# Loads of 64-bit weights by GpSimd's queue, a third merged attention block, and the last 512 tokens in two runs

## The chip, the cores and the metric

One core of a Trainium2 chip runs the whole program in one launch. The metric is the time of one execution on the device in microseconds, as the median of several runs. The engines are TensorE (PE, matmuls; its weight loads are PEld), VectorE (DVE), ScalarE (ACT), GpSimd (POOL) and SyncE (SP, which here only issues transfers).

## The reference, cut to what matters

```python
# r, k, v, w: (2, 8, 768, 48); u: (8, 48); all float32
for t in range(768):                                   # per batch and head
    y[t]  = r[t] @ (state + outer(u * k[t], v[t]))
    state = w[t][:, None] * state + outer(k[t], v[t])
x = y as (1536 tokens, 384)
h = x @ w_in                  # 384 -> 2048; w_in, w_out are float64
x = (h * sigmoid(h)) @ w_out  # 2048 -> 384
P = exp(logits - max), logits = x @ w_gate             # 8 experts
8 times: P /= P.sum(1); P /= P.sum(0); P *= 1536 / 8
out = sum over e of P[:, e] * (relu(x @ w1[e]) @ w2[e])  # 384 -> 1024 -> 384
```

## The kernel before, in words

**Attention** goes in 24 units: 6 blocks of 256 tokens (three for each batch entry) times 4 pairs of heads; unit i is block i // 4, pair i % 4. A unit has four parts: `attn_a` (decay products by scans on VectorE), `attn_b` (scores on TensorE, masked on VectorE), `attn_c` (states) and `attn_d` (outputs y on TensorE, copied by ScalarE at line 338 and sent by DMA to the block's x1). Units below NS = 8, the first two blocks, take a merged form: one scan (line 296) over a unit's four chunk states, whose multipliers, the decay operands `tot`, ScalarE writes at line 291; all else on VectorE and ScalarE. Units 8 and up take a plain form: four chained steps (line 313), two products (line 316), more and smaller instructions on VectorE, and two products on GpSimd (lines 194, 204).

**First dense layer.** 2048 hidden columns are 16 f-tiles. The first 512 tokens are steps 0 to 15, tokens 512 to 1023 two runs of 256 (steps 16 to 31 and 32 to 47), the last 512 tokens steps 48 to 63. Step s runs `m_l1` (9 matmuls and silu; line 476 forms the remainder of g on VectorE) and `m_l2` of step s - 2 (9 matmuls). Every float32 operand is split into a rounded part and a remainder, so each product takes three matmuls.

**Weights.** w_in and w_out are float64 and come as pairs of 32-bit words, in 32 pieces of 384 columns. SP issues each into one of four raw buffers. `narrow` makes float32 of it by three integer operations on VectorE (lines 127, 129, 130); ScalarE rounds (line 104) and VectorE, or GpSimd for pieces 8 to 31, subtracts (line 106). A gate (line 82) is a one-element copy on ScalarE into a raw buffer out of a unit's x tile, so that the transfer behind it waits for parts b of units 4, 5 and 6. Expert weights (64 pieces of 768 columns, float32) use the same buffers.

**Order.** The program is written in the order of `run`: units 0 to 7 first, then the steps, with pieces split by `wcurve` and attention parts by `curve`. x1 of blocks 2, 3, and 4 and 5 together is split at steps 16, 32 and 48. Each engine's order comes from a scheduler in the compiler that goes by this order where it can. Each engine then works in order. In the expert phase (192 steps of 21 matmuls) `w_range` reads w and the double weights again to test their range, one part a step.

Of the kernel before, what the change touches and what calls it, by code (L numbers as in the profile page):

```python
# [5 lines left out]
F32 = mybir.dt.float32  # L6
F32R = mybir.dt.float32r
# [19 lines left out]
LN = 64 + D  # L27
NS = 2 * NP
C_MASK = 0
# [25 lines left out]
class Pipeline:  # L55
# [4 lines left out]
    def setup_weights(self):  # L60
        self.pieces = []
        win, wout, w1, w2 = (self.ins[n] for n in ("moe_w_in", "moe_w_out", "moe2_w1", "moe2_w2"))
        for f in range(16):
            for kind, src in (("a", win), ("b", wout)):
                self.pieces.append((kind, f // 8, f % 8, src[:, f * HP:(f + 1) * HP].bitcast(I32)))
        for e in range(E):
            for j in range(4):
                for kind, src in (("a", w1), ("b", w2)):
                    self.pieces.append((kind, 2 + e, 2 * j, src[e][:, j * PIECE:(j + 1) * PIECE]))
        self.n_dma = self.n_split = 0  # L70
        self.raw, self.wt, self.gates = {}, {}, {}

    def dma_pieces(self, n):
        nc = self.nc
        n = min(n, len(self.pieces))
        while self.n_dma < n:
            i = self.n_dma
            src = self.pieces[i][3]
            t = self.raw_p.tile([128, PIECE], F32, tag="raw", name="raw")
            gate = self.gates.get(i)  # L80
            if gate is not None:
                nc.scalar.copy(t[0:1, 0:1], gate)
            nc.sync.dma_start(out=t.bitcast(I32) if i < N64 else t, in_=src)
            self.raw[i] = t
            self.n_dma += 1

    def split_pieces(self, n):
        nc = self.nc
        n = min(n, len(self.pieces))
        while self.n_split < n:  # L90
            i = self.n_split
            self.dma_pieces(i + 1)
            kind, u, f, _ = self.pieces[i]
            raw = self.raw.pop(i)
            if i >= N64 or f % 2 == 0:
                pool = self.wa_p if kind == "a" else self.wb_p
                self.wt[kind, u, f // 2] = (pool.tile([128, PIECE], F32R, tag="hi", name="whi"),
                                            pool.tile([128, PIECE], F32R, tag="lo", name="wlo"))
            hi, lo = self.wt[kind, u, f // 2]
            if i < N64:  # L100
                o = (f % 2) * HP
                hi, lo = hi[:, o:o + HP], lo[:, o:o + HP]
                raw = self.narrow(i, raw)
            nc.scalar.copy(hi, raw)  # L104
            eng = nc.vector if i < N64 and not K['wl_pool'][0] <= i < K['wl_pool'][1] else nc.gpsimd
            eng.tensor_sub(lo, raw, hi.bitcast(F32))  # L106
            self.n_split += 1
            self.dma_pieces(self.n_split + 3)

    def narrow(self, i, raw):  # L110
# [60 lines left out]
    def attn_a(self, i):  # L171
# [7 lines left out]
        d1 = self.d1[i % 2]  # L179
        if i == 2:  # L180
            zek = self.aux[0:LN, 0:2 * WPAD + BLK]
            zf, ef = (zek[:, o:o + WPAD].rearrange("p (c t) -> p c t", c=4) for o in (0, WPAD))
            kz = zek[:, 2 * WPAD:].rearrange("p (c t) -> p c t", c=4)
        else:
            zf = self.sc_p.tile([LN, 4, CH + 2], F32, tag="zf", name="zf")
            ef = self.sc_p.tile([LN, 4, CH + 2], F32, tag="ef", name="ef")
            kz = self.sc_p.tile([LN, 4, CH], F32, tag="kz", name="kz")
        zff = zf.rearrange("p c t -> p (c t)")
# [31 lines left out]
    def attn_b(self, i):  # L220
        nc = self.nc
        if i < NS:
            self.warm(K['wm'])
# [49 lines left out]
    def attn_c(self, i):  # L273
        nc = self.nc
        blk, p = divmod(i, NP)
        b, q = divmod(blk, BPS)
        if i < NS:
            self.warm(K['wm'])
# [4 lines left out]
        if i < NS:  # L283

            uv = self.attn_bank("u", i)[0:LN, 0:6 * D].rearrange("p (e c) -> p e c", c=6)
            for c in range(4):
                for lo in (0, 64):
                    nc.tensor.matmul(uv[lo:lo + D, :, c + 1], lhsT=kt[lo:lo + 64, c, :], rhs=lv[lo:lo + 64, 1, c, :],
                                     start=True, stop=True)
            tot = self.tot[i % 2]  # L290
            nc.scalar.copy(tot[:, :, 0:4], st["zf"][:, :, 1].rearrange("p (o c) -> p o c", o=1).to_broadcast([LN, D, 4]))
            if q == 0:
                nc.vector.memset(uv[:, :, 0], 0.0)
            else:
# [24 lines left out]
    def attn_d(self, i):  # L319
# [21 lines left out]
        for s in range(2):  # L341
            for off, n, c, pp in dense_runs(2 * p + s):
                (nc.scalar if i < NS else nc.sync).dma_start(out=self.x1[blk][pp:pp + n, c, :], in_=ys[64 * s + off:64 * s + off + n, :])
        if p > 0 and blk < 2:
# [20 lines left out]
    def attn_x(self, i):  # L365
        return self.x[i % 4 if i < NS else i % 2]

    def attn_bank(self, kind, i):
        if i < NS and i % 2:
            return self.banks[{"m": 0, "u": 3, "y": 4}[kind]]  # L370
# [17 lines left out]
    def attn_tiles(self):  # L388
        self.d1 = [self.ac_p.tile([LN, 4, CH + 2], F32, name=f"d1{j}") for j in range(2)]
        self.x = [self.ac_p.tile([128, 2, 4, CH], F32, name=f"x{j}") for j in range(2)]  # L390
        xx = self.x2_p.tile([128, 2, 2, 4, CH], F32, name="xx", tag="x2_1")
# [3 lines left out]
        o = 2 * WPAD + BLK  # L395
        self.tot = [self.aux[0:LN, o + j * 6 * D:o + (j + 1) * 6 * D].rearrange("p (e c) -> p e c", c=6) for j in range(2)]
        self.oneb = self.ac_p.tile([128, 128], F32R, name="oneb")
# [199 lines left out]
    def w_range(self):  # L597
        nc = self.nc
        sm = self.sm_p
        n = NT * DM // (128 * PIECE)  # L600
        mm = sm.tile([128, 2, n], F32, name="wmm")
        for i in range(n):
            t = self.raw_p.tile([128, PIECE], F32, tag="raw", name="wt")
            nc.sync.dma_start(out=t, in_=self.ins["w"][:, i * PIECE:(i + 1) * PIECE])
            yield
# [11 lines left out]
        for i in range(N64):  # L617
            t = self.raw_p.tile([128, PIECE], F32, tag="raw", name="wh64")
            nc.sync.dma_start(out=t.bitcast(I32), in_=self.pieces[i][3])
# [19 lines left out]
    def run(self):  # L639
        tc, nc = self.tc, self.nc  # L640
        with ExitStack() as ctx:
# [16 lines left out]
            self.wb_p = pool("wb", 8)  # L658
            self.raw_p = pool("raw", 4)
            self.x2_p = pool("x2", 1)  # L660
# [37 lines left out]
            ticks.sort(key=lambda t: (t[2] >= NS, t[0], -t[2]))  # L698
            pos = [0]

            def attn_to(n):
                while not gen and pos[0] < len(ticks) and (ticks[pos[0]][2] < NS or ticks[pos[0]][0] < n):
                    _, fn, i = ticks[pos[0]]
# [24 lines left out]
            x1_at = {6: 2, 12: 3, 28: 4, 38: 5}  # L728
            split_at = {16: (2,), 32: (3,), 48: (4, 5)}

# [7 lines left out]
            for i in range(len(steps) + 2):  # L738
                if i < len(steps):
                    s = steps[i]  # L740
                    if s[0] == "m":
# [9 lines left out]
                        attn_to(at(curve, i + 1))  # L751
                        if tb == 2:
                            if f == 0:
# [13 lines left out]
                if i >= 2:  # L767
                    s = steps[i - 2]
                    if s[0] == "m":
                        _, tb, o, n, f = s  # L770
                        self.m_l2(tb, o, n, f)
                        if f == 15 and tb == 2:
                            self.logits(2)
# [86 lines left out]
```

## Time and profile before

| | us |
|---|---|
| median of 3 runs (1153.33 to 1156.07) | 1155.81 |
| the profiled execution | 1154.07 |
| its span, first to last instruction | 1152.3 |
| TensorE busy | 1115.0 |
| VectorE, ScalarE, GpSimd busy | 494.7, 319.5, 185.4 |
| first matmul of step 16, of step 32, of the expert phase | 161.3, 208.3, 332.7 |

A row of the order of time has the start and the duration in us, the engine and line, the operation, the tiles (out<-in, buffer numbers left out) and shapes; in brackets the idle time of the engine ahead of it and what ended it. Matmuls are pipelined, so that their durations overlap and only the distance of their starts tells their price. A clock of 1.00 is 2.4 GHz, 0.50 is 1.2 GHz.

### The profile page before, as it was taken

How to read it: one execution, taken by the hardware profiler on the slowest of the kernel's cores; microseconds unless marked ns; L12 is line 12 of the kernel's file. 1: busy time of each engine (PE TensorE's matmuls, PEld its weight loads, DVE VectorE, ACT ScalarE, POOL GpSimd, SP SyncE). 2: the span in 40 equal slices, each digit the busy share in tenths (PEclk: the TensorE clock that was granted, in tenths of full speed). 3: DMA queues.
4: the chain of work that ended last, by engine and by line, in shares of the span. 5: the costliest groups of instructions: out<-in, count | busy, mean ns of one | idle time of the engine just before them, and what ended most of it. 6: DMA issues, size and time to landing. Idle time of an engine off the chain costs nothing.

```text
span 1152.3 us, 16926 instructions
## 1 busy us (share of the span) xinstructions
PE 1115.0 (97%) x6928; PEld 989.9 (86%) x6928; DVE 494.7 (43%) x985; ACT 319.5 (28%) x613; POOL 185.4 (16%) x137
## 2 busy tenths in 40 slices
PE   7778999998999999999999999999999999999997
PEld 7656789996888999999999999899999999899996
DVE  7699967894233321222224522432442253222221
ACT  3243334444541243113112311311331241111110
POOL 0136511211440031004003100400310040000000
PEclk8659999999999999999999999999999999999999
DMA  5565512211230021003103400510340050000000
GB/s 139 163 194 155 154 44 72 74 43 49 83 84 13 1 56 54 1 15 83 42 1 101 133 1 17 150 53 1 94 126 1 23 159 26 1 1 1 28 28 30
DMA packets 32087, 71.81 MB, mean 62 GB/s; under 512 B 4752, under 2 KB 11904, under 8 KB 32000
## 3 DMA queue, kind: packets, MB, share of 16 engines
q1 hardware_dynamic: 30912, 69.86, 21.4%
q8 instruction: 56, 0.92, 0.3%
q10 hardware_dynamic: 1088, 0.79, 0.2%
q14 instruction: 31, 0.25, 0.1%
HBM read 65.91 MB, written 2.36 MB: 59 GB/s over the span
## 4 chain that ended last, share of the span: by engine, by line
PE 76%; ACT 0%; DVE 0%; issue 0%; DVEq 0%
PE bank L579 12%; PE bank L581 12%; PE bank L563 12%; PE bank L564 12%; PE bank L580 12%; PE bank L562 11%; PE bank L487 1%; PE bank L468 1%; PE bank L489 1%; PE bank L488 1%; PE bank L469 1%; PE bank L470 1%; ACT x2h L522 0%; DVE acc L592 0%; PE bank L507 0%; PE bank L549 0%
## 5 line engine op out<-in xcount | busy, mean ns | idle before, releaser
L568 DVE SCALAR_TENSOR_TENSOR hl<-bank,hh 128x512 fp32r<-128x512 f32 x192 | 132.2, 689 | 413.4 <-ACT hh L567 413.3
L579 PE MATMUL bank<-whi,hh 128*128 128x384 f32 x768 | 258.8, 337 | 0.0
L580 PE MATMUL bank<-wlo,hh 128*128 128x384 f32 x768 | 258.4, 336 | 0.0
L581 PE MATMUL bank<-whi,hl 128*128 128x384 f32 x768 | 257.6, 337 | 0.0
L567 ACT ACTIVATE hh<-bank 128x512 fp32r<-128x512 f32 x192 | 114.4, 596 | 483.1 <-PE bank L564 476.3
L564 PE MATMUL bank<-x2h,wlo 128*128 128x512 f32 x576 | 228.0, 396 | 0.0
L563 PE MATMUL bank<-x2l,whi 128*128 128x512 f32 x576 | 227.4, 395 | 0.0
L562 PE MATMUL bank<-x2h,whi 128*128 128x512 f32 x576 | 224.3, 389 | 0.0
L106 POOL TENSOR_TENSOR wlo<-raw,whi 128x768 fp32r<-128x768 f32 x64 | 119.4, 1870 | 579.3 <-ACT whi L104 551.2
L579 PEld LDWEIGHTS bank<-whi,hh 128*128 128x128 f32 x768 | 144.3, 188 | 9.2 <-issue 0.6
L580 PEld LDWEIGHTS bank<-wlo,hh 128*128 128x128 f32 x768 | 144.2, 188 | 8.0
L581 PEld LDWEIGHTS bank<-whi,hl 128*128 128x128 f32 x768 | 144.1, 188 | 1.4
L564 PEld LDWEIGHTS bank<-x2h,wlo 128*128 128x128 f32 x576 | 108.0, 188 | 22.4
L563 PEld LDWEIGHTS bank<-x2l,whi 128*128 128x128 f32 x576 | 108.0, 188 | 17.4
L562 PEld LDWEIGHTS bank<-x2h,whi 128*128 128x128 f32 x576 | 108.2, 188 | 17.0
L104 ACT CAST whi<-raw 128x768 fp32r<-128x768 f32 x64 | 53.6, 837 | 90.7 <-PE bank L563 54.1
L468 PE MATMUL bank<-x1h,whi 128*128 128x512 f32 (+1 forms) x192 | 68.1, 359 | 7.3 <-ACT x1h L357 7.3
L592 DVE SCALAR_TENSOR_TENSOR acc<-bank,P,acc 128x384 f32<-128x384 f32 x84 | 47.8, 610 | 58.0 <-PE bank L581 58.0
L469 PE MATMUL bank<-x1l,whi 128*128 128x512 f32 (+1 forms) x192 | 67.9, 353 | 0.3 <-DVE x1l L358 0.3
L488 PE MATMUL bank<-gl,whi 128*128 128x512 f32 (+1 forms) x192 | 66.4, 346 | 1.4 <-DVE gl L476 1.4
L470 PE MATMUL bank<-x1h,wlo 128*128 128x512 f32 (+1 forms) x192 | 67.4, 351 | 0.0
L476 DVE TENSOR_TENSOR gl<-g,gh 128x512 fp32r<-128x512 f32 (+1 forms) x64 | 44.2, 693 | 53.4 <-ACT gh L475 37.6
(163 smaller groups left out, 1176.5 us busy)
## 6 DMA issues: line engine op xcount, KB each, us to landing
raw<-in_moe_w_dram SPq DMA_DIRECT2D x64, 384.0 KB, 3.2
at<-in_att_dram SPq DMA_DIRECT2D x16, 484.0 KB, 3.6
raw<-in_moe_w_in_dram SPq DMA_DIRECT2D x16, 384.0 KB, 3.4
raw<-in_moe_w_out_dram SPq DMA_DIRECT2D x16, 384.0 KB, 3.4
wh<-in_moe_w_in_dram SPq DMA_DIRECT2D x16, 384.0 KB, 3.2
wh<-in_moe_w_out_dram SPq DMA_DIRECT2D x16, 384.0 KB, 3.2
at<-in_att_dram SPq DMA_DIRECT2D x7, 339.5 KB, 3.7
wt<-in_w_dram SPq DMA_DIRECT2D x6, 384.0 KB, 3.2
```

Of the source, the lines that this page charges most:

```text
L106: eng.tensor_sub(lo, raw, hi.bitcast(F32))
L468: nc.tensor.matmul(ps, lhsT=wh, rhs=xh[:, d, :], start=(d == 0), stop=False)
L469: nc.tensor.matmul(ps, lhsT=wh, rhs=xl[:, d, :], start=False, stop=False)
L470: nc.tensor.matmul(ps, lhsT=wl, rhs=xh[:, d, :], start=False, stop=(d == 2))
L562: nc.tensor.matmul(ps, lhsT=wh, rhs=xh[:, d, :], start=(d == 0), stop=False)
L563: nc.tensor.matmul(ps, lhsT=wh, rhs=xl[:, d, :], start=False, stop=False)
L564: nc.tensor.matmul(ps, lhsT=wl, rhs=xh[:, d, :], start=False, stop=(d == 2))
L567: nc.scalar.activation(hh, ps, ACTF.Relu)
L568: nc.vector.scalar_tensor_tensor(hl, ps, 0.0, hh.bitcast(F32), op0=ALU.max, op1=ALU.subtract)
L579: nc.tensor.matmul(ps, lhsT=hh[:, sl], rhs=wh, start=st, stop=False)
L580: nc.tensor.matmul(ps, lhsT=hh[:, sl], rhs=wl, start=False, stop=False)
L581: nc.tensor.matmul(ps, lhsT=hl[:, sl], rhs=wh, start=False, stop=sp)
```

## The change

The double weights come in 16 pieces of 768 columns. GpSimd issues their loads and makes the gate copies, now behind parts b of units 3 and 5. They have three raw buffers: two of the pool and one that takes the place of the decay operands (tag x2_0); expert weights share the pool's two in pairs. All 16 remainders are formed on VectorE. The third block (units 8 to 11) takes the merged form; the first two blocks have four decay operands instead of two, the third block one of its own. The last 512 tokens are two runs of 256, with x1 of blocks 4 and 5 split at steps 48 and 64, and attention spread accordingly. The range test reads in pieces of 1536 columns and starts one expert later.

```diff
-NS = 2 * NP
+N4 = 2 * NP
+NS = 3 * NP
-N64 = 32
-HP = PIECE // 2
+N64 = 16
-K = {'tk': (4, 0, 2, 4, 6), 'wr': (3, 0), 'wl_pool': (8, 32), 'wm': 1, 'gate': (4, 5, 6)}
+K = {'tk': (4, 0, 2, 4, 6), 'wr': (4, 0), 'wm': 1, 'gate': (3, 5)}
...
-            t = self.raw_p.tile([128, PIECE], F32, tag="raw", name="raw")
-            gate = self.gates.get(i)
-            if gate is not None:
-                nc.scalar.copy(t[0:1, 0:1], gate)
-            nc.sync.dma_start(out=t.bitcast(I32) if i < N64 else t, in_=src)
+            if i < N64:
+                if i % 3 < 2:
+                    t = self.raw_p.tile([128, 2, PIECE], F32, tag="raw", name="raw")
+                else:
+                    if i == 2:
+                        self.raw64 = self.x2_p.tile([128, 2, PIECE], F32, tag="x2_0", name="raw")
+                    t = self.raw64
+                gate = self.gates.get(i)
+                if gate is not None:
+                    nc.gpsimd.tensor_copy(t[0:1, 0, 0:1], gate)
+                nc.gpsimd.dma_start(out=t.rearrange("p s n -> p (s n)").bitcast(I32), in_=src)
+            else:
+                if i % 2 == 0:
+                    self.raw2 = self.raw_p.tile([128, 2, PIECE], F32, tag="raw", name="raw")
+                t = self.raw2[:, i % 2]
+                nc.sync.dma_start(out=t, in_=src)
...
-            eng = nc.vector if i < N64 and not K['wl_pool'][0] <= i < K['wl_pool'][1] else nc.gpsimd
-            eng.tensor_sub(lo, raw, hi.bitcast(F32))
+            (nc.vector if i < N64 else nc.gpsimd).tensor_sub(lo, raw, hi.bitcast(F32))
             self.n_split += 1
-            self.dma_pieces(self.n_split + 3)
+            self.dma_pieces(self.n_split + 2)
...
-            tot = self.tot[i % 2]
+            tot = self.tot[i % 4 if i < N4 else 4]
...
-        self.tot = [self.aux[0:LN, o + j * 6 * D:o + (j + 1) * 6 * D].rearrange("p (e c) -> p e c", c=6) for j in range(2)]
+        self.tot = [self.aux[0:LN, j * 6 * D:(j + 1) * 6 * D].rearrange("p (e c) -> p e c", c=6) for j in range(4)] + [late]
...
-        n = NT * DM // (128 * PIECE)
+        n = NT * DM // (128 * 2 * PIECE)
...
-            for tb, o, n in ((0, 0, 512), (1, 0, 256), (1, 256, 256), (2, 0, 512)):
+            for tb, o, n in ((0, 0, 512), (1, 0, 256), (1, 256, 256), (2, 0, 256), (2, 256, 256)):
...
-            curve = [(0, 32), (15, 51), (31, 67), (46, 104), (NM, 104)]
-            wcurve = [(0, 6), (13, 32), (NM, 32)]
-            split_at = {16: (2,), 32: (3,), 48: (4, 5)}
+            curve = [(0, 32), (15, 51), (31, 67), (47, 83), (63, 104), (NM, 104)]
+            wcurve = [(0, 4), (13, 16), (NM, 16)]
+            split_at = {16: (2,), 32: (3,), 48: (4,), 64: (5,)}
```

Elsewhere tests of `i < NS` that choose banks, x tiles, warm-up matmuls, the queue of x1's stores and the order of parts become `i < N4`.

## Rows read from the trace of the kernel before

**Rows 1.** Windows by stage: length, busy (count) by engine, PEclk, DMA share, GB/s.
```profile
34.00:80.00 46.00, 32.44 (x374) 25.34 (x371) 38.12 (x87) 15.23 (x43) 10.31 (x13) 0.59 0.64 193
80.00:161.00 81.00, 74.72 (x432) 57.40 (x430) 70.19 (x137) 32.49 (x65) 37.74 (x29) 0.92 0.44 129
161.00:208.00 47.00, 47.00 (x503) 43.60 (x503) 35.44 (x85) 19.36 (x52) 7.48 (x8) 1.00 0.21 61
208.00:260.00 52.00, 52.00 (x656) 48.51 (x655) 47.26 (x127) 21.86 (x62) 9.32 (x12) 1.00 0.21 61
260.00:277.00 17.00, 13.29 (x99) 9.15 (x98) 8.84 (x19) 7.54 (x16) 1.84 (x1) 0.90 0.05 13
344.00:1148.00 804.00, 800.44 (x4046) 724.61 (x4038) 249.79 (x445) 178.48 (x296) 88.97 (x49) 1.00 0.16 44
```
**Rows 2.** VectorE in order of time: start, duration, line, tiles, idle time before.
```profile
23.32 0.76 DVE L296 TENSOR_TENSOR_SCAN ss<-bank,aux 112x288 f32<-112x288 f32 x1
...
27.78 0.76 DVE L296 TENSOR_TENSOR_SCAN ss<-bank,aux 112x288 f32<-112x288 f32 x1
...
35.68 0.36 DVE L127 TENSOR_SCALAR cv<-raw 128x384 int32<-128x384 int32 x1 [3.25 <-DMA raw<-in_moe_w_in_dram]
...
45.09 0.36 DVE L127 TENSOR_SCALAR cv<-raw 128x384 int32<-128x384 int32 x1 [3.50 <-DMA raw<-in_moe_w_out_dram]
...
46.03 0.75 DVE L296 TENSOR_TENSOR_SCAN ss<-bank,aux 112x288 f32<-112x288 f32 x1
...
66.65 0.75 DVE L296 TENSOR_TENSOR_SCAN ss<-bank,aux 112x288 f32<-112x288 f32 x1
...
77.97 1.23 DVE L358 TENSOR_TENSOR x1l<-x,x1h 128x256 fp32r<-128x256 f32 x1
```
**Rows 3.** ScalarE in order of time, unit 4's end and unit 5's gate.
```profile
41.32 0.19 ACT L82 COPY raw<-x 1x1 f32<-1x1 f32 x1 [2.03 <-DVE x L264]
41.41 0.36 ACT L338 COPY ys<-bank 112x256 f32<-112x256 f32 x1
```
**Rows 4.** VectorE's groups from 0 to 260 us: count, busy us, mean ns, idle.
```profile
L130 DVE SCALAR_TENSOR_TENSOR cv<-raw,cv 128x384 int32<-128x384 int32 x32 | 20.7, 651 | 0.1
...
L129 DVE SCALAR_TENSOR_TENSOR cv<-raw,cv 128x384 int32<-128x384 int32 x32 | 18.9, 598 | 0.3
...
L127 DVE TENSOR_SCALAR cv<-raw 128x384 int32<-128x384 int32 x32 | 14.1, 446 | 10.8 <-DMA raw<-in_moe_w_in_dram 4.7 <-DMA raw<-in_moe_w_out_dram 3.5 <-POOL wlo L106 2.6
...
L476 DVE TENSOR_TENSOR gl<-g,gh 128x256 fp32r<-128x256 f32 x31 | 13.3, 429 | 5.4 <-ACT gh L475 5.3
...
L106 DVE TENSOR_TENSOR wlo<-cv,whi 128x384 fp32r<-128x384 f32 x8 | 4.3, 542 | 0.0
```
**Rows 5.** Single lines: count, shortest/median/longest ns, first and last start.
```profile
L127 DVE TENSOR_SCALAR cv<-raw x32: 323/348/1175, 35.7 to 127.5; 128x384 int32<-128x384 int32 x32
...
L130 DVE SCALAR_TENSOR_TENSOR cv<-raw,cv x32: 532/545/1381, 37.3 to 132.4; 128x384 int32<-128x384 int32 x32
...
L106 POOL TENSOR_TENSOR wlo<-raw,whi x64: 1835/1846/2271, 274.9 to 949.6; 128x768 fp32r<-128x768 f32 x64
L106 POOL TENSOR_TENSOR wlo<-cv,whi x24: 997/1120/6118, 69.0 to 135.7; 128x384 fp32r<-128x384 f32 x24
```
**Rows 6.** TensorE in order of time: steps 14, 16 and 21.
```profile
150.71 0.39 PE L468 MATMUL bank<-x1h,whi 128*128 128x512 f32 x1
...
152.53 0.39 PE L470 MATMUL bank<-x1h,wlo 128*128 128x512 f32 x1
...
161.30 0.39 PE L468 MATMUL bank<-x1h,whi 128*128 128x256 f32 x1
...
188.19 0.28 PE L468 MATMUL bank<-x1h,whi 128*128 128x256 f32 x1
...
189.15 0.28 PE L470 MATMUL bank<-x1h,wlo 128*128 128x256 f32 x1
```
**Rows 7.** DMA issues: count, KB each, median us to landing.
```profile
raw<-in_moe_w_in_dram SPq DMA_DIRECT2D x16, 384.0 KB, 3.4
```

More of the change, by code (lines that the diff above doesn't have):

```diff
@@ L62, in setup_weights @@
         win, wout, w1, w2 = (self.ins[n] for n in ("moe_w_in", "moe_w_out", "moe2_w1", "moe2_w2"))
-        for f in range(16):
+        for g in range(8):
             for kind, src in (("a", win), ("b", wout)):
-                self.pieces.append((kind, f // 8, f % 8, src[:, f * HP:(f + 1) * HP].bitcast(I32)))
+                self.pieces.append((kind, g // 4, 2 * (g % 4), src[:, g * PIECE:(g + 1) * PIECE].bitcast(I32)))
         for e in range(E):
@@ L179, in attn_a @@
         d1 = self.d1[i % 2]
[L180 to L187, printed above, removed]
+        zf = self.sc_p.tile([LN, 4, CH + 2], F32, tag="zf", name="zf")
+        ef = self.sc_p.tile([LN, 4, CH + 2], F32, tag="ef", name="ef")
+        kz = self.sc_p.tile([LN, 4, CH], F32, tag="kz", name="kz")
         zff = zf.rearrange("p c t -> p (c t)")
@@ L221, in attn_b @@
         nc = self.nc
-        if i < NS:
+        if i < N4:
             self.warm(K['wm'])
@@ L342, in attn_d @@
             for off, n, c, pp in dense_runs(2 * p + s):
-                (nc.scalar if i < NS else nc.sync).dma_start(out=self.x1[blk][pp:pp + n, c, :], in_=ys[64 * s + off:64 * s + off + n, :])
+                (nc.scalar if i < N4 else nc.sync).dma_start(out=self.x1[blk][pp:pp + n, c, :], in_=ys[64 * s + off:64 * s + off + n, :])
         if p > 0 and blk < 2:
@@ L365, in attn_x @@
     def attn_x(self, i):
-        return self.x[i % 4 if i < NS else i % 2]
+        return self.x[i % 4 if i < N4 else i % 2]
     def attn_bank(self, kind, i):
-        if i < NS and i % 2:
+        if i < N4 and i % 2:
             return self.banks[{"m": 0, "u": 3, "y": 4}[kind]]
@@ L390, in attn_tiles @@
         self.x = [self.ac_p.tile([128, 2, 4, CH], F32, name=f"x{j}") for j in range(2)]
-        xx = self.x2_p.tile([128, 2, 2, 4, CH], F32, name="xx", tag="x2_1")
+        xx = self.x2_p.tile([128, 3 * 512], F32, name="xx", tag="x2_1")
+        late = xx[0:LN, 1024:1024 + 6 * D].rearrange("p (e c) -> p e c", c=6)
+        xx = xx[:, 0:1024].rearrange("p (j s c t) -> p j s c t", j=2, s=2, c=4)
         self.x += [xx[:, 0], xx[:, 1]]
@@ L599, in w_range @@
         sm = self.sm_p
-        n = NT * DM // (128 * PIECE)
+        n = NT * DM // (128 * 2 * PIECE)
         mm = sm.tile([128, 2, n], F32, name="wmm")
         for i in range(n):
-            t = self.raw_p.tile([128, PIECE], F32, tag="raw", name="wt")
-            nc.sync.dma_start(out=t, in_=self.ins["w"][:, i * PIECE:(i + 1) * PIECE])
+            t = self.raw_p.tile([128, 2 * PIECE], F32, tag="raw", name="wt")
+            nc.sync.dma_start(out=t, in_=self.ins["w"][:, i * 2 * PIECE:(i + 1) * 2 * PIECE])
             yield
@@ L617, in w_range @@
         for i in range(N64):
-            t = self.raw_p.tile([128, PIECE], F32, tag="raw", name="wh64")
+            t = self.raw_p.tile([128, 2 * PIECE], F32, tag="raw", name="wh64")
             nc.sync.dma_start(out=t.bitcast(I32), in_=self.pieces[i][3])
@@ L658, in run @@
             self.wb_p = pool("wb", 8)
-            self.raw_p = pool("raw", 4)
+            self.raw_p = pool("raw", 2)
             self.x2_p = pool("x2", 1)
@@ L697, in run @@
                     ticks.append((K["tk"][0] * i + o, fn, i))
-            ticks.sort(key=lambda t: (t[2] >= NS, t[0], -t[2]))
+            ticks.sort(key=lambda t: (t[2] >= N4, t[0], -t[2]))
             pos = [0]
             def attn_to(n):
-                while not gen and pos[0] < len(ticks) and (ticks[pos[0]][2] < NS or ticks[pos[0]][0] < n):
+                while not gen and pos[0] < len(ticks) and (ticks[pos[0]][2] < N4 or ticks[pos[0]][0] < n):
                     _, fn, i = ticks[pos[0]]
@@ L751, in run @@
                         attn_to(at(curve, i + 1))
-                        if tb == 2:
+                        if tb == 2 and o == 256:
                             if f == 0:
@@ L771, in run @@
                         self.m_l2(tb, o, n, f)
-                        if f == 15 and tb == 2:
+                        if f == 15 and tb == 2 and o == 256:
                             self.logits(2)
```

23 lines of the change are left out of this document (9 added, 14 removed).

## The prediction

> **What bounds the kernel now.** I read the page first, then the busy times by stage, then the order of work on single engines where a stage loses time. By stage [rows 1]: from 344 to 1148 us TensorE is busy 800.4 of 804 us at the full clock. That is the expert phase, and of it the change touches only the loads of raw weights and the range test, both off TensorE. I leave it as it is. All that can move lies ahead of 344 us. From 161 to 260 us TensorE is busy without a break; from 260 to 277 it is idle for 3.7 us and its granted clock is 0.90. From 34 to 80 us it is busy 32.4 of 46 us at a clock of 0.59 (a mixture of 1.2 and 2.4 GHz), and from 80 to 161 us VectorE is busy 70.2 of 81. So the front is held by a chain through VectorE, the middle by TensorE, and one seam (260 to 277) by a wait.
>
> The front's chain is seen in VectorE's order of work [rows 2]. Each merged attention unit ends its state in one scan of line 296. Units 2 and 3 finish 4.46 us apart (23.32, 27.78). Then unit 5 comes only at 46.03 and unit 7 at 66.65: four gaps of 9.72 on average. The cause stands between them: VectorE, which works in order, sits 3.25 and 3.50 us before line 127, waiting for a piece of double weights that has not landed. ScalarE adds to it [rows 3]: its gate copy of line 82 waits 2.03 us for VectorE's select of the next unit, and the copy of y (line 338) that ends the unit before stands behind it. Only after unit 7 can the first 512 tokens be complete: its x1 remainder ends at 77.97 + 1.23 = 79.2 us, 12.55 us after the scan began. From there to the start of step 16 (161.3, [rows 6]) are 82 us for the first 512 tokens.
>
> **The sum is made** against the profiled execution: 1154.07 us, a span of 1152.3 and 1.8 around it. The median of the three runs is 1.7 us more, which I add at the end. A measurement of this kernel tells from no change about 0.3%, 3.5 us.
>
> **Part 1: gates and loads by GpSimd, the third buffer, four decay operands (first two blocks).** The gate copies leave ScalarE. Of sixteen pieces only two can be on their way before unit 7's scan: the third buffer is the memory of the four decay operands (tag x2_0) and comes free with that scan, and on GpSimd's queue piece 3 stands behind piece 2. So VectorE can be held at most twice in units 4 to 7. If nothing held it, unit 7's scan would begin at 27.78 + 4 x 4.46 = 45.6 us. If the conversion of both pieces falls inside the chain, it costs two times 3.25 us (next part): 52.1. If VectorE also waits 3.4 us for each of the two landings, as it did [rows 2]: 58.9. I take 52, because attention stands first in program order but pieces fill gaps, and no gate holds ScalarE any more. The gain is 66.65 - 52 = 14.6 us, with bounds 7.7 and 21. The four decay operands end a wait of ScalarE that only mattered between units; I count it as nothing, since VectorE is the slower there. Loads on SP (attention inputs, x1 stores) no longer queue behind waits for raw buffers; nothing in the rows shows that they were late, so nothing.
>
> **Part 2: wider pieces, remainder on VectorE.** Per half piece VectorE now does 0.35 (line 127), 0.54 and 0.54 us undisturbed [rows 5] but 0.45, 0.60 and 0.65 on average [rows 4], since GpSimd's subtractions (24 of them, 1.12 us each at the median, [rows 5]) run beside it and single instructions stretch to 1.38 us. All narrowing and 8 subtractions: 14.1 + 18.9 + 20.7 + 4.3 = 58.0 us. For 768 columns: a subtraction takes 0.43 us for 256 columns and 0.54 for 384 [rows 4], so some 0.9 us for 768; lines 129 and 130 have 384's time in common with it, so 0.9 each; line 127 between 0.35 and 0.70, I take 0.55. A piece is 0.55 + 3 x 0.9 = 3.25 us, sixteen are 52.0: 6 less than now, though all subtractions move to VectorE. The upper bound is two halves each, 2 x (0.35 + 3 x 0.54) = 3.9 us, 63 in all, 5 more than now. GpSimd's 24 subtractions vanish, and with them the stretching of other instructions.
>
> **Part 3: third block merged.** A plain unit costs VectorE at most 5.4 us: (47.26 - 16 x 0.43 for g's remainders - 6 x 0.43 for x1's) / 7 units from 208 to 260 us [rows 1, 4]. A merged one is at most 4.46 [rows 2], its share of x1's remainder with it, so some 4.1. Four units save 5 us. TensorE pays: a plain unit is (52.0 - 16 x 2.16) / 8 = 2.2 us; a merged one issues 48 matmuls by the code where a plain one issues 28, so between 2.2 and 2.2 x 48 / 28 = 3.8; I take 3.2, 4 us more in all.
>
> **Parts 1 to 3 together, the first 512 tokens.** They are complete at 52 + 12.6 = 64.6 us (now 79.2). From there TensorE needs 16 x 4.1 (18 matmuls 0.2275 us apart, [rows 6]) + 4 x 3.2 = 78 us. VectorE needs 13 pieces (three are done by then), 42 us, 16 remainders of g at 0.65 (worked out as above for 512 columns), 10, four merged units, 16, and 3 us of the next: 72. TensorE's floor is now 65.6 + 8.8 = 74, of which the measured 82 is 8 more. After: 78 plus 2, since VectorE no longer lags as much; 80, with bounds 78 and 88 (the same 8 and the upper price of Part 2). That is 2 us less (bounds -4 and +6). The transfers are covered: a half piece lands 3.4 us after issue [rows 7], 193 GB/s went through at a busy share of 0.64 [rows 1], and three buffers turn around in 15 us at 5 us a piece. If the cover is gone, see the slower rival.
>
> **Part 4: last 512 tokens as two runs, attention spread to step 63.** A 256-column step costs 18 x 0.12 = 2.16 us, a 512-column one 4.1 [rows 6]: two for one cost 0.24 more, sixteen times 3.84 us. The wait at step 48 goes: 3.7 us idle, and (1 - 0.90) x 17 = 1.7 us of clock, 5.4 together. Attention of the last two blocks only moves, its TensorE time is the same. What is late next are the seams: unit 19's last part is issued in step 46 for a need in step 48, unit 23's in step 58 for step 64. Net -1 us; bounds -1.6 (all of it) and +7 (a wait of 3 us at both seams on top of 3.84). The expert weights are now split in 16 steps of 2.16 us; GpSimd's 8 subtractions of 1.85 us [rows 5] fit in 35 us. Expert phase with two raw buffers of pairs, and half as many range-test loads: nothing, covered by TensorE; VectorE is busy 250 of 804 us there.
>
> **Sum.** 1154.07 - 14.6 - 2 - 1 = 1136.5, plus 1.7: 1138 us. Its own range, half of the parts' bounds added up (-3.2 - 1 - 0.3 and +3.5 + 4 + 4): 1133 to 1150.
>
> **The rivals.**
> A, landings still hold VectorE, and longer. Place: lines 127 of pieces 0 and 1, ahead of scans 4 to 7. For it: twice the bytes per piece, on a queue that this trace has no transfer of. Against it: two holds instead of three or more, and ScalarE free. Scan at 59 instead of 52, so 1138 + 7 = 1145 us.
> On this hold the Trainium skill, "SBUF — State Buffer", section "SBUF: two separate sides", speaks against the change: a transfer issued from GpSimd has its descriptors written by that engine, and VectorE's two-port operations lock it out meanwhile. With its figures (620 ns becoming 3100) two landings are 5 us later, an estimate that would make 1143; line 127's 0.35 beside 0.54 for the same width [rows 5] fits such an operation, but no run here shows a load so issued.
> B, the floor is reached: no piece falls inside the chain and TensorE runs at its need. 1154.07 - 21 - 4 - 1.6 + 1.7 = 1129 us. For it: VectorE's clean 4.46 us for two units in a row. Against: pieces 0 and 1 do land before unit 7.
> C, the seams at 48 and 64 wait as now: Part 4 becomes +7, 1146 us. For it: the copies between y and x1 are unchanged. Against: half the attention per step.
> D, the slower side: transfers bound the first 512 tokens. Place: pieces 2 to 15, issued in order by GpSimd, each only when one of three buffers is free. Fourteen pieces from 52 us on must be done by about step 14, now at 150.7 [rows 6]; so it decides from (150.7 - 52) / 14 = 7.0 us a piece, that is 21 us around for each of three buffers. Less 3.25 us of conversion that is a landing of about 18 us, where [rows 7] have 3.4 for half the bytes. At 8 us a piece step 14 starts at 164, 13 us later than now, and the time is 1155.8 + 13 - 1 = 1168 us. For it: a queue that this trace doesn't show. Against it: a factor of five.
> That the change doesn't do what it says, three buffers from the start, I have taken for certain: the third comes with unit 7's scan.
>
> **How the numbers follow.** Forecast 0.46, A 0.20, B 0.16, C 0.10, D 0.08. Faster by over 0.3% (under 1152.3): all of B, nearly all of the forecast, four fifths of A and C; with room for mishaps 0.83. Within: 0.10. Slower: D, 0.07. The range reaches down to B with a merged unit at TensorE's lower price (-4) and a better clock than 0.59 in what is left of the front (-4), and up to the forecast's own upper end and a little of A and C beyond it: 1121 to 1153.
>
> **What would show it.** Scans of line 296 for units 4 to 7 some 5 to 6 us apart, the eighth near 52; no line 82 on ScalarE; step 16's first matmul near 145 us; no stretched lines 129 and 130; the expert phase starting near 315 (now 332.7, as the table above has it) and lasting as long. It is wrong if those scans stay 9 us apart, if TensorE waits for a split piece after 70 us, or if the expert phase shows idle time.

## Result and the profile after

The changed kernel takes 1143.84 us (median of 4 runs, 1142.99 to 1145.63); the kernel before, run beside it, 1154.76. The ratio is 0.9908, 95% interval 0.9889 to 0.9927. The profiled execution took 1143.81 us, with a span of 1142.0. The forecast was 1138.0: direction and range held, and the gain is 10.9 us in place of 17.6 (14.6 + 2 + 1). The sum under it came out very differently from its terms.

Line numbers have moved. Line 127 (first narrowing instruction) is now 134, 129 and 130 are 136 and 137, 106 (the remainder) is 113, the scan's 296 is 298, g's remainder 476 is 479, and the raw loads' 83 is 90.

Stages of the two profiled executions, in us; "complete" is the end of the last x1 remainder of the first 512 tokens:

| | before | after |
|---|---|---|
| eighth scan | 66.7 | 64.0 |
| first 512 tokens complete | 79.2 | 74.3 |
| from there to step 16 | 82.1 | 75.9 |
| step 16's first matmul | 161.3 | 150.2 |
| first expert matmul | 332.7 | 324.3 |
| step 16 to the end | 991.0 | 991.8 |

So all of the gain is there at step 16: 11.1 us, 4.9 ahead of completion and 6.2 behind it. The busy times by stage of the changed kernel, with the columns of [rows 1], show the same:

```profile
34.00:74.00 40.00, 27.25 (x410) 23.14 (x410) 26.05 (x48) 10.91 (x28) 3.60 (x7) 0.68 0.54 163
74.00:150.00 76.00, 76.00 (x618) 61.05 (x620) 64.27 (x110) 36.24 (x66) 11.73 (x18) 0.96 0.47 153
...
243.00:288.00 45.00, 45.00 (x484) 42.05 (x484) 28.69 (x73) 19.81 (x51) 2.76 (x4) 1.00 0.04 12
288.00:324.00 36.00, 36.00 (x316) 35.16 (x315) 14.86 (x20) 23.04 (x49) 24.29 (x13) 1.00 0.39 115
324.00:1142.00 818.00, 810.62 (x4095) 732.66 (x4094) 246.56 (x398) 182.28 (x290) 93.86 (x52) 1.00 0.14 46
```

From 74 us on TensorE never stands still before the expert phase; in the kernel before it was idle for 6.3 us of the 81 ahead of step 16. The seam at step 48 is gone too. Only the front (34 to 74) is still a chain through VectorE. Its order of work there, which answers to [rows 2] (start, duration, engine, line, in brackets the idle time ahead and what ended it):

```profile
28.68 0.76 DVE L298 TENSOR_TENSOR_SCAN ss<-bank,aux 112x288 f32<-112x288 f32 x1
33.09 0.56 DVE L134 TENSOR_SCALAR cv<-raw 128x768 int32<-128x768 int32 x1 [3.65 <-DMA raw<-in_moe_w_in_dram]
...
39.59 0.73 DVE L298 TENSOR_TENSOR_SCAN ss<-bank,aux 112x288 f32<-112x288 f32 x1
45.12 0.73 DVE L298 TENSOR_TENSOR_SCAN ss<-bank,aux 112x288 f32<-112x288 f32 x1
...
51.67 0.56 DVE L134 TENSOR_SCALAR cv<-raw 128x768 int32<-128x768 int32 x1 [4.74 <-DMA raw<-in_moe_w_out_dram]
57.23 0.53 DVE L134 TENSOR_SCALAR cv<-raw 128x768 int32<-128x768 int32 x1
...
63.98 0.76 DVE L298 TENSOR_TENSOR_SCAN ss<-bank,aux 112x288 f32<-112x288 f32 x1 [1.04 <-ACT bank L297]
...
69.61 0.56 DVE L134 TENSOR_SCALAR cv<-raw 128x768 int32<-128x768 int32 x1 [2.55 <-DMA raw<-in_moe_w_in_dram]
```

VectorE still stands before line 134 for a piece that has not landed, and longer than before: 3.65 and 4.74 us (3.25 and 3.50 in [rows 2]). GpSimd's order of work tells why. It has taken the place of ScalarE's gate in [rows 3]:

```profile
43.52 0.50 POOL L89 COPY raw<-x 1x1 f32<-1x1 f32 x1 [16.12 <-DVE x L266]
43.97 1.05 POOL L90 DMA_DIRECT2D raw<-in_moe_w_out_dram  x2
...
65.03 0.53 POOL L90 DMA_DIRECT2D raw<-in_moe_w_in_dram  x1 [3.94 <-DVE ss L298]
```

The gate lets pieces 1 and 3 go at 43.97. Piece 1 is there 7.7 us later, at 51.67, and VectorE's queue had reached its conversion at 46.9. Piece 3 goes with it, ahead of piece 2 (the prediction had the two the other way round on GpSimd's queue), so that its conversion, at 57.23, is the third ahead of the eighth scan. Piece 2, in the third buffer, goes only at 65.03, after the eighth scan, and holds VectorE at 69.61.

The conversions and remainders, which answer to [rows 5] (duration in ns as minimum, median and maximum):

```profile
L134 DVE TENSOR_SCALAR cv<-raw x16: 529/548/561, 33.1 to 123.8; 128x768 int32<-128x768 int32 x16
...
L137 DVE SCALAR_TENSOR_TENSOR cv<-raw,cv x16: 925/948/961, 35.3 to 127.3; 128x768 int32<-128x768 int32 x16
...
L113 DVE TENSOR_TENSOR wlo<-cv,whi x16: 928/946/1358, 37.6 to 129.6; 128x768 fp32r<-128x768 f32 x16
```

A piece is 0.55 + 3 x 0.95 = 3.4 us, sixteen are 54 (forecast: 3.25 and 52.0). No narrowing is stretched any more; [rows 5] had maxima of 1175 and 1381.

### The profile page after: what moved, and what is told of

Read it like the earlier page. It is cut to its first block, busy times and chain, and to the rows that moved or that the text cites. A ratio compares the mean times of both kernels' runs of the same rounds, so it can differ in the third digit from the quotient of the medians.

```text
span 1142.0 us, 17576 instructions
## 1 busy us (share of the span) xinstructions
PE 1112.4 (97%) x7392; PEld 1004.2 (88%) x7392; DVE 476.3 (42%) x877; ACT 322.8 (28%) x615; POOL 153.4 (13%) x129
## 4 chain that ended last, share of the span: by engine, by line
PE 90%; DMA 3%; DVE 3%; issue 1%; ACT 0%; POOL 0%; ACTq 0%; SPq 0%; DVEq 0%; POOLq 0%
PE bank L582 11%; PE bank L584 11%; PE bank L583 11%; PE bank L566 11%; PE bank L567 11%; PE bank L565 11%; PE bank L490 3%; PE bank L471 3%; PE bank L492 3%; PE bank L491 3%; PE bank L472 3%; PE bank L473 3%; PE bank L233 1%; DMA at<-in_att_dram 1%; PE bank L338 1%
## 5 line engine op out<-in xcount | busy, mean ns | idle before, releaser
L584 PE MATMUL bank<-whi,hl 128*128 128x384 f32 x768 | 254.2, 337 | 0.0
L471 PE MATMUL bank<-x1h,whi 128*128 128x256 f32 (+1 forms) x240 | 75.0, 314 | 2.8 <-ACT x1h L359 2.8
L490 PE MATMUL bank<-gh,whi 128*128 128x256 f32 (+1 forms) x240 | 74.7, 317 | 0.0
L472 PE MATMUL bank<-x1l,whi 128*128 128x256 f32 (+1 forms) x240 | 73.9, 309 | 0.0
L473 PE MATMUL bank<-x1h,wlo 128*128 128x256 f32 (+1 forms) x240 | 73.6, 308 | 0.0
L492 PE MATMUL bank<-gh,wlo 128*128 128x256 f32 (+1 forms) x240 | 73.1, 306 | 0.0
```

What stands on the lines that cost most here:

```text
L471: nc.tensor.matmul(ps, lhsT=wh, rhs=xh[:, d, :], start=(d == 0), stop=False)
L472: nc.tensor.matmul(ps, lhsT=wh, rhs=xl[:, d, :], start=False, stop=False)
L490: nc.tensor.matmul(ps, lhsT=wdh, rhs=gh, start=first, stop=False)
L584: nc.tensor.matmul(ps, lhsT=hl[:, sl], rhs=wh, start=False, stop=sp)
```

## Experiments

Ratios are to the kernel before on the same chip, with a 95% interval; stage times are of one profiled execution each. Two questions were open: which part carries the gain, and why the attention chain gave so little of its share.

**Remainders of pieces 4 to 15 back on GpSimd** (e6_pool)

```diff
-            (nc.vector if i < N64 else nc.gpsimd).tensor_sub(lo, raw, hi.bitcast(F32))
+            (nc.vector if i < 4 else nc.gpsimd).tensor_sub(lo, raw, hi.bitcast(F32))
```

> The kernel after with the weight remainders of pieces 4 to 15 formed on GpSimd again (part of part 2 undone); the first four stay on VectorE. Theory C (GpSimd's subtractions stretch VectorE's instructions, so that giving them to VectorE costs nothing): VectorE's lines 136 and 137 stretch from 0.95 us to over 1.3 in places, step 16 comes 3 to 8 us later, 1146 to 1152 us; the loads on GpSimd's queue also wait for its subtractions. Rival: VectorE is relieved of 12 x 0.95 = 11 us and step 16 comes up to 5 us earlier, 1139.

1154.12 us, 0.9995 (0.9986 to 1.0003): the whole gain is gone, as theory C has it, and by more than its range. The front is not touched (complete at 72.8), but step 16 comes at 159.7, 9.5 us later than in the changed kernel. Durations by source, and TensorE's waits from 74 to 161 us:

```profile
L136 DVE SCALAR_TENSOR_TENSOR cv<-raw,cv x16: 927/955/2748, 32.7 to 128.9; 128x768 int32<-128x768 int32 x16
...
L113 POOL TENSOR_TENSOR wlo<-cv,whi x12: 1815/1980/3107, 78.1 to 133.0; 128x768 fp32r<-128x768 f32 x12
```

```profile
PE bank L240 <- DVE ss L298: 5.2, 1, 5.2
PE bank L491 <- DVE gl L479: 1.8, 1, 1.8
PE bank L471 <- ACT g L477: 1.8, 1, 1.8
```

Twelve instructions on another engine stretch VectorE's from 0.95 to as much as 2.75 us, and TensorE waits three times, 8.8 us in all: twice for VectorE (7.0) and once for ScalarE. The loads on GpSimd's queue are not the cause: VectorE waits only 0.6 us for pieces from 74 to 161 us.

**The kernel before, with its 24 GpSimd remainders on VectorE** (e9_b_dvesub)

```diff
-K = {'tk': (4, 0, 2, 4, 6), 'wr': (3, 0), 'wl_pool': (8, 32), 'wm': 1, 'gate': (4, 5, 6)}
+K = {'tk': (4, 0, 2, 4, 6), 'wr': (3, 0), 'wl_pool': (32, 32), 'wm': 1, 'gate': (4, 5, 6)}
```

> The kernel before, with one edit: the 24 subtractions of pieces 8 to 31 that GpSimd does (line 106) go to VectorE; half pieces, ScalarE's gates, SP's loads and the plain third block stay. If GpSimd's subtractions themselves are what the first 512 tokens lost (they stretch VectorE's instructions and end late), most of Part 2's gain comes from this word alone: VectorE gets 24 x 0.54 = 13 us more work but loses the stretching, step 16's first matmul some 4 to 8 us earlier than in before, 1146 to 1150 us. If the wider pieces are needed with it (32 x (0.35 + 3 x 0.54) = 63 us of VectorE in place of 58.0), VectorE, busy 70.2 of 81 us there, fills up: step 16 at 161 or later, 1153 to 1160 us.

1144.42 us, 0.9907 (0.9892 to 0.9921), better than either expectation: this one edit gives what the whole change gives. Busy times by stage, and a source row:

```profile
80.00:151.00 71.00, 71.00 (x450) 55.85 (x451) 67.14 (x164) 33.34 (x66) 24.66 (x8) 0.97 0.48 146
```

```profile
L129 DVE SCALAR_TENSOR_TENSOR cv<-raw,cv x32: 518/549/559, 35.8 to 130.0; 128x384 int32<-128x384 int32 x32
```

The front is the one of before (eighth scan 66.7, complete 79.7). From there to step 16 (149.9) are 70.2 us in place of 82.1, with TensorE busy throughout. VectorE's conversions now take 32 x (0.35 + 3 x 0.55) = 64 us, more than the 58.0 of before, and its busy share is 95%, and yet everything is earlier. What was lost in the kernel before is seen in its own rows: VectorE's order of work, GpSimd's and TensorE's, and two windows of 4 us with the columns of [rows 1].

```profile
109.16 0.35 DVE L127 TENSOR_SCALAR cv<-raw 128x384 int32<-128x384 int32 x1
109.43 1.38 DVE L130 SCALAR_TENSOR_TENSOR cv<-raw,cv 128x384 int32<-128x384 int32 x1
110.73 0.54 DVE L129 SCALAR_TENSOR_TENSOR cv<-raw,cv 128x384 int32<-128x384 int32 x1
```

```profile
109.39 1.01 POOL L106 TENSOR_TENSOR wlo<-cv,whi 128x384 fp32r<-128x384 f32 x1 [1.04 <-ACT whi L104]
```

```profile
116.46 0.39 PE L256 MATMUL bank<-qh,oneb 112*128 112x256 f32 x1 [3.42 <-DVE ss L313]
...
118.56 0.63 PE L489 MATMUL bank<-gh,wlo 128*128 128x512 f32 x1
118.99 0.63 PE L487 MATMUL bank<-gh,whi 128*128 128x512 f32 x1
```

```profile
107.00:111.00 4.00, 4.00 (x13) 3.10 (x12) 4.00 (x7) 1.96 (x5) 2.01 (x2) 0.57 0.63 173
117.00:121.00 4.00, 4.00 (x12) 2.64 (x12) 3.94 (x8) 1.87 (x5) 3.16 (x2) 0.57 0.69 223
```

While GpSimd's remainder ran from 109.39 to 110.40, the 0.55 us of line 130 became 1.38. TensorE then waited 3.42 us for VectorE (1.40 at 106.31 as well), and behind each of the two waits the granted clock was lower: 0.57 of full speed from 107 to 111 and from 117 to 121 us, matmuls 0.43 us apart where they were 0.23 (most of it at 1.2 GHz). In the kernel before TensorE was idle for 6.3 us (81.0 - 74.72) of the stretch in [rows 1]; here for none of 71. With (1 - 0.57) x 8 = 3.4 us of clock that is 9.7 of the 11.9 us. The scheduler has also put VectorE's instructions into another order in this run; what of the 11.9 us is due to that no run tells apart.

The Trainium skill, "SBUF — State Buffer", section "SBUF: two separate sides", says that the port pair shared by GpSimd and VectorE is an exclusive lock against VectorE instructions with two SBUF inputs: who comes second waits for the whole instruction. The row of line 130, which reads two such inputs, agrees: it ends 0.41 us after GpSimd's remainder. One such wait doesn't account for GpSimd's 6.12 us in [rows 5]: the longest instruction of VectorE beside it took 0.69 us.

**Third block plain again** (e5_plain3)

```diff
-NS = 3 * NP
+NS = 2 * NP
```

> The kernel after with the third block in the plain form again (part 3 undone). By the prediction's part 3 VectorE gets 5 us more and TensorE 4 us less between the completion of the first 512 tokens (74.3 us) and step 16 (150.2). The trace after shows TensorE without idle time from 74 to 150, so theory F (TensorE's need is the floor there): step 16 comes 0 to 4 us earlier, 1140 to 1144 us. Rival V (VectorE's work is the floor there): step 16 comes 3 to 7 us later, 1147 to 1151.

1147.71 us, 0.9928 (0.9916 to 0.9941). Step 16 is at 153.8, 3.6 us later, in rival V's range. So the merged block is worth some 4 us inside this change. But VectorE's work is not the floor, since it waits; the mechanism is seen on GpSimd and, behind it, on VectorE:

```profile
90.25 9.68 POOL L206 TENSOR_TENSOR x<-at,ef 48x256 f32<-48x256 f32 x1 [3.42 <-DVE ef L198]
99.89 0.59 POOL L90 DMA_DIRECT2D raw<-in_moe_w_out_dram  x1
```

```profile
106.49 0.56 DVE L134 TENSOR_SCALAR cv<-raw 128x768 int32<-128x768 int32 x1 [7.11 <-DMA raw<-in_moe_w_out_dram]
```

A plain unit has a product on GpSimd (line 206) that took 0.68 us at best. Beside dense VectorE work it took 9.68; the loads of raw pieces stood behind it in the same queue, and VectorE then waited 7.11 us for a piece. With the merged block the first of these products comes at 130.1, here at 45.1. That the queue behind the product counts, and not the product, e9_b_dvesub shows, where SP issues the loads: there one of GpSimd's products (line 194) took 13.15 us at 87.18, and TensorE was never idle.

**Last 512 tokens in one run** (e4_tail512)

```diff
-            for tb, o, n in ((0, 0, 512), (1, 0, 256), (1, 256, 256), (2, 0, 256), (2, 256, 256)):
+            for tb, o, n in ((0, 0, 512), (1, 0, 256), (1, 256, 256), (2, 0, 512)):
...
-            curve = [(0, 32), (15, 51), (31, 67), (47, 83), (63, 104), (NM, 104)]
+            curve = [(0, 32), (15, 51), (31, 67), (46, 104), (NM, 104)]
```

> The kernel after with the last 512 tokens in one run again and attention and splits as before (part 4 undone). By the prediction's part 4 (two runs cost 3.84 us and save a wait of 5.4): 1 to 2 us slower than the kernel after, 1145. By what the traces show now (step 16 to the expert phase took 171.4 us before and 174.1 after, with TensorE never idle after): 2 to 3 us faster, 1141. Should the wait at step 48 be smaller here than 5.4 us, since attention is ahead, faster by more, down to 1138.

1142.1 us, 0.9888 (0.9872 to 0.9905). Step 16 to the end is 990.6 us, 991.8 with the two runs. The intervals overlap: Part 4 is worth nothing that can be told.

**One gate, behind unit 7** (e1_gate7), and **no gate** (e2_nogate)

```diff
-K = {'tk': (4, 0, 2, 4, 6), 'wr': (4, 0), 'wm': 1, 'gate': (3, 5)}
+K = {'tk': (4, 0, 2, 4, 6), 'wr': (4, 0), 'wm': 1, 'gate': (7,)}
```

(and `'gate': ()`).

> The kernel after with one gate behind part b of unit 7 in place of the two behind units 3 and 5, so that no load of double weights is on its way while units 4 to 7 run. Theory 1 (VectorE, in order, stands before pieces that have not landed; 3.65 and 4.74 us in the kernel after, and the chain of units waits with it): the eighth scan of line 298 begins near 46 to 48 us (63.98 in the kernel after), the first 512 tokens are complete near 57, step 16 starts at 135 to 141, the time is 1129 to 1135 us. Rival 1 (the conversions only move behind the attention, and VectorE becomes the bound of the first 512 tokens): the same scan, but step 16 not before 146, 1140 us or more.

> The kernel after without gates: pieces 0 and 1 are issued at the start and land long before they are converted. Theory 1: no idle time before line 134 ahead of unit 7's scan; that scan begins near 46 + 3 x 3.4 = 56 us (three conversions stand inside the chain) plus what the attention loads lose to 1.5 MB of early weights, up to 5 us; 1136 to 1141 us. Rival 2 (the landing does not matter, the conversions inside the chain do): the scan stays at 62 to 64 and the time at 1143 to 1145.

With the one gate 1140.85 us, 0.9879 (0.9859 to 0.9898). No piece is converted inside the chain: eighth scan at 52.3, and complete at 67.5, 6.8 us earlier than with the change. So theory 1 missed its 46 to 48: even without pieces the last four units are 5.96 us apart (28.45 to 52.30), and VectorE is idle for 9.7 of these 23.9 us, the longest times for ScalarE (2.91) and for attention inputs (2.24). Step 16 (146.7) is only 3.5 us earlier, as rival 1 has it. VectorE's order of work and the stages behind it:

```profile
52.30 0.76 DVE L298 TENSOR_TENSOR_SCAN ss<-bank,aux 112x288 f32<-112x288 f32 x1 [2.91 <-ACT bank L297]
54.42 0.56 DVE L134 TENSOR_SCALAR cv<-raw 128x768 int32<-128x768 int32 x1 [1.36 <-DMA raw<-in_moe_w_out_dram]
...
63.75 0.56 DVE L134 TENSOR_SCALAR cv<-raw 128x768 int32<-128x768 int32 x1 [2.35 <-DMA raw<-in_moe_w_out_dram]
```

```profile
54.00:68.00 14.00, 7.47 (x79) 5.82 (x76) 11.16 (x18) 4.17 (x9) 1.06 (x2) 0.63 0.83 294
68.00:147.00 79.00, 76.16 (x579) 60.70 (x577) 66.72 (x109) 37.09 (x65) 16.59 (x20) 0.96 0.48 153
```

Half of the front's gain goes: completion to step 16 takes 79.2 us in place of 75.9, with TensorE idle for 2.8 of them. Without any gate: 1139.92, 0.987 (0.9854 to 0.9887). Its six executions spread from 1138.42 to 1145.80, and the profiled one took 1145.31, so that its stages need not be those of the median. In it no piece holds VectorE ahead of the eighth scan, which is at 63.8 (complete at 75.1) all the same: the early loads bring the first scan at 19.9 instead of 14.0, and three conversions stand ahead of the eighth. By their time the gate's worth can't be told: the first interval overlaps the changed kernel's (0.9889 to 0.9927), the second ends just below it.

**Gates behind units 1 and 2** (e7_gate12), and the same with piece 2 in the pool (e8_p2gate12)

```diff
-K = {'tk': (4, 0, 2, 4, 6), 'wr': (4, 0), 'wm': 1, 'gate': (3, 5)}
+K = {'tk': (4, 0, 2, 4, 6), 'wr': (4, 0), 'wm': 1, 'gate': (1, 2)}
...
-                if i % 3 < 2:
+                if i % 3 < 2 or i == 2:
...
-                    if i == 2:
+                    if i == 5:
```

(the first edit alone is e7_gate12).

> The kernel after with the gates behind parts b of units 1 and 2 instead of 3 and 5: pieces 0 and 1 are issued near 17 and 21 us, behind the first attention loads. Theory 1: no hold over 1 us before line 134 ahead of the eighth scan, which begins near 46 + 2 x 3.4 = 53 us; but the third piece still waits for that scan, so the gain against the kernel after is 3 to 6 us: 1138 to 1141. Rival (early loads delay the attention loads as without gates, where the first scan came at 19.9 instead of 14.0 us): the scan stays at 60 or later, 1142 or more.

> As the run with gates behind units 1 and 2, and piece 2 comes into the pool's two buffers, so that the buffer in place of the decay operands is first used by piece 5. Theory 1 with VectorE's work as what is left: four or five pieces are converted before the eighth scan, which comes near 46 + 4.5 x 3.4 = 61 us, but few are left behind it; step 2 at 73 to 76, step 16 at 143 to 146, 1134 to 1138 us. Rival F (TensorE's need from the completion of the first 512 tokens is all that counts): step 16 = completion + 76; with completion at 71, 147, 1141 us.

Theory 1 missed in both. With the gates alone 1143.65 us, 0.9899 (0.9885 to 0.9914), eighth scan at 63.8, though the first scan, at 13.6, is not delayed: the first hold only comes earlier (4.41 us at 23.8). With piece 2 as well 1151.11 us, 0.9957 (0.9942 to 0.9972): more pieces are converted inside the chain, the eighth scan is at 72.8, complete at 83.4. The eighth scan goes with the number of pieces converted ahead of it: none, 52.3 (e1_gate7); three, 63.8 to 64.0 (this run with the gates alone, the run without gates, the changed kernel) or 59.3 where the holds are short (e3_spq, below); six, 72.8.

**Loads by SP in place of GpSimd** (e3_spq)

```diff
-                nc.gpsimd.dma_start(out=t.rearrange("p s n -> p (s n)").bitcast(I32), in_=src)
+                nc.sync.dma_start(out=t.rearrange("p s n -> p (s n)").bitcast(I32), in_=src)
```

> The kernel after with the loads of double weights issued by SP instead of GpSimd (gates still copied by GpSimd). Theory 1 (the gate sets when the load starts, the queue hardly matters): the eighth scan between 60 and 64 us, landings of 4 to 5 us as now, 1141 to 1146 us. Rival 3 (GpSimd's queue makes the early landings long, 7.6 us for piece 1): landings under 4.5 us, the scan near 58, 1138 us or less.

1141.81 us, 0.9898 (0.9873 to 0.9923); median landings 5.0 and 4.4 us, where GpSimd's queue had 5.0 and 4.6. The queue makes no difference to the time that can be told. The front does differ: VectorE is held 1.46 and 1.66 us for pieces 0 and 1 (3.65 and 4.74 with the change), and the eighth scan, with three conversions ahead of it here too, is at 59.3, near rival 3's 58. On SP piece 3 left at 38.50 and piece 1, behind its gate, at 41.37; on GpSimd both left together behind the gate, and piece 1 took 7.7 us. At completion only 1.0 us of it is left (73.3 for 74.3). What made piece 1 late was the transfers themselves: from 47 to 50 us the changed kernel's DMA engines were at a busy share of 1.00 (414 GB/s), with pieces 1 and 3 and an attention load (issued at 47.42) under way at once, and VectorE did nothing. The hold of the Trainium skill's sentence in rival A (descriptors locked out) is not seen.

**Combinations** (e10_gate7_tail512, e11_gate7_spq): the edits of the runs named, with the one gate behind unit 7.

> The changed kernel with two edits that each showed no loss alone: one gate, behind the attention of unit 7, and the last 512 tokens in one run of 16 steps. If both add up, 1139 to 1141 us, 3 to 5 us under the changed kernel; if the front's gain is taken back at the seam of step 48 (more of the last two blocks' attention must be done by then), as much as the changed kernel, 1142 to 1145.

> The changed kernel with one gate, behind unit 7, and the double weights' loads issued by SP. If the queue matters once all three buffers are asked for at once (GpSimd spends some 0.5 us on each issue), 1138 to 1140 us; if not, as with the gate alone, 1140 to 1143.

1138.19 us, 0.985 (0.9832 to 0.9868), and 1139.15, 0.9876 (0.9858 to 0.9895). The first beats both kernels; its interval lies below the changed kernel's. The second can't be told from the gate alone (0.9859 to 0.9898). The first is complete at 67.9, at step 16 at 144.7, and takes 990.2 us from there.

**The kernel before with the remainders on VectorE and one gate behind unit 7** (e12_b_dvesub_gate7)

```diff
-K = {'tk': (4, 0, 2, 4, 6), 'wr': (3, 0), 'wl_pool': (8, 32), 'wm': 1, 'gate': (4, 5, 6)}
+K = {'tk': (4, 0, 2, 4, 6), 'wr': (3, 0), 'wl_pool': (32, 32), 'wm': 1, 'gate': (7,)}
```

> The kernel before with two edits: the 24 subtractions to VectorE, as in the run that showed 1144.42, and one gate, behind the attention of unit 7, in place of three behind units 4 to 6. The attention chain should then be free of holds: eighth scan near 46 to 52 in place of 66.7, the first 512 tokens complete at 60 to 67. If VectorE's work is what bounds the way to step 16 (63 us of conversions, nearly all of it now behind the chain, and 10 of remainders of g), most of this is given back: step 16 at 145 to 149, 1140 to 1144 us. If TensorE's need bounds it (70.2 us from completion to step 16 in the run without this gate), step 16 comes at 131 to 137 and the time is 1126 to 1132.

1148.26 us, 0.9937 (0.9922 to 0.9953), slower than without the second edit and outside both forecasts. The front is as clean as hoped (eighth scan 52.5, complete 62.4), 17.3 us ahead of e9_b_dvesub, and step 16 is at 159.5, 9.6 us behind it. TensorE's waits from 62 to 160 us, and GpSimd's order of work:

```profile
PE bank L468 <- ACT whi L104: 7.3, 4, 3.9
PE bank L232 <- POOL x L204: 4.1, 1, 4.1
```

```profile
74.67 5.33 POOL L194 TENSOR_TENSOR kz<-at,zf 112x256 f32<-112x256 f32 x1 [19.30 <-issue]
...
102.01 6.24 POOL L204 TENSOR_TENSOR x<-at,ef 48x256 f32<-48x256 f32 x1 [4.44 <-DVE ss L313]
```

The conversions are late (the last remainder ends at 158.5, 137.5 without the gate), and the plain units' products on GpSimd take 5.33 and 6.24 us beside VectorE. How much of the 27 us is due to which is not told apart; the 13.15 us of such a product in e9_b_dvesub cost TensorE nothing.

## Why the prediction was right in sign and in range, and wrong in its terms

**Part 1 was mis-sized, and it is the step that failed.** "I take 52" for the eighth scan, 14.6 us: measured 2.7 (64.0), and 4.9 at completion. The prediction started from 45.6 for a chain that nothing holds, added two conversions, 6.5 us, and no wait, since "pieces fill gaps". All three failed. The gate behind unit 7 showed that 52.3 is what the chain takes with no piece in it, 6.7 us more than 45.6. Three pieces were converted ahead of the scan and not two, 3.4 us each, since piece 3 was issued ahead of piece 2. And VectorE works in order: a conversion placed before a scan holds it until the piece lands, and the gate lets the load go too late for that, so rival A came true beyond its own 59, with two holds of 8.4 us together (6.8 priced). By the prediction's own sign of being wrong ("if those scans stay 9 us apart") this part failed as well: the last four units are (63.98 - 28.68) / 4 = 8.8 us apart. The step had its root in the reading of [rows 2], which show two holds; the trace of before has nine half pieces converted ahead of the eighth scan (line 127, 35.68 to 64.44), some 18 us by the prediction's own price.

**Parts 1 to 3 together were mis-sized the other way.** "That is 2 us less" measured 6.2. The prediction saw the cause, GpSimd's subtractions and the stretching, but priced it by VectorE's sum alone (58.0 to 52.0 us). The run of before with the remainders on VectorE raised that sum to 64 and still took 11.9 us off the same stretch: what cost time was TensorE waiting for stretched instructions, and the clock behind those waits. A sum of one engine's busy time can't show that. The floor of TensorE was miscounted too. "16 x 4.1" is 288 matmuls behind completion; the traces of before and after have 256 there, since 14 of the first layer's run earlier and the second layer's last 18 only behind step 16's first matmul. At 0.2275 us that is 58.2 in place of 65.6, so that the floor of before was 67 and not 74, and 15 us could be won and not 8. The forecast's 78 came near the 75.9 measured, all of them busy, because what stood beside the matmuls, the merged units and the clock (0.96), was priced too low.

**Part 2's prices held** (3.4 us a piece for 3.25), and so did the cover of the transfers: rival D did not come, and TensorE waits for no piece after 70 us. **Part 3**: its own worth, by undoing it, is 4 us where the forecast counted VectorE's -5 against TensorE's +4. By the rows it came from GpSimd's products and the loads behind them, which the merged block keeps out of most of the stretch and the prediction had not priced. **Part 4**: forecast -1, measured +2.7 from step 16 to the expert phase (171.4 to 174.1) and +0.8 to the end; the wait at step 48 went and the finer steps took it back. Rival C did not come. The **expert phase** lasted about as long: 819.6 and 817.7 us from its first matmul; where the 1.9 us came from no run shows.

That the sum fell into its range is in part luck: of the profiled span the forecast had 14.6, 2 and 1, measured were 4.9, 6.2 and -0.8, and the misses partly cancel.

So the time fell by 10.9 us mainly because the remainders left GpSimd (9.5 us at step 16 when undone), and little because of the chain: with the remainders back on GpSimd the earlier completion leaves 1.6 us at step 16 (159.7 for 161.3). The rest of the change nets nothing against that one edit in the kernel before: 0.9908 and 0.9907. It completes the first 512 tokens 5.4 us earlier than that kernel and needs 5.7 us more from there to step 16. TensorE is busy throughout in both, so those 5.7 us are its own work: 618 matmuls in the stretch shown above for the one, 450 for the other, as the merged units issue more (the clock was 0.96 and 0.97). What remains open is which of the wider pieces and GpSimd's queue makes the plain block slower with the change (78.6 us to step 16 in e5_plain3, 70.2 in e9_b_dvesub). The rows of e5_plain3 speak for the queue; a plain third block with loads by SP was not run.

## What to carry to other kernels

When two engines' instructions stretch each other, price the waits of the engine behind them, not the sum of busy time: moving work onto an engine that was busy for 87% of a stretch made the stretch 11.9 us shorter, because the partner that slowed this engine was gone. In an in-order queue a conversion that is put ahead of a critical instruction costs its duration, and its load's landing on top unless that was issued early enough; look at the issue time, not only at the landing time. Issuing earlier has its price as well: without gates the first scan came 5.9 us later. And where steps overlap, count what lies between two marks in the trace, not what a step holds. Before crediting a change of four parts, try its cheapest edit alone in the old kernel.

## What the runs showed of the hardware that was not expected

GpSimd suffers more than VectorE where both read two operands. Elementwise products of 0.69 us took 13.15 (e9_b_dvesub), 9.68 (e5_plain3), 6.24 and 5.33 us (e12_b_dvesub_gate7) beside dense VectorE work, and a remainder 6.12 in the kernel before (median 1.12, [rows 5]); VectorE's line 136 went from 0.95 to at most 2.75. Each of these four products ended 0.5 to 0.6 us after VectorE had run out of work for the first time since the product began (100.33 and 99.77, 99.93 and 99.39, 108.24 and 107.71, 80.00 and 79.51): they waited for a pause, not for one instruction. Two others (6.54 us in e9_b_dvesub, 6.59 in e5_plain3) ended without one. What stands behind such an instruction on GpSimd's queue, loads among it, waits as well.
